# A fused attention, mixer and FFN kernel: centring in three passes, the low part of the sum of squares apart, one inverse root moved

## The chip, the cores and the metric

The kernel runs on one core of a Trainium2 chip, as one launch. The metric is the device time in microseconds (us); lower is better. The engines are called PE (TensorE, matrix products), DVE (VectorE), ACT (ScalarE), POOL (GpSimd) and SP (SyncE, which issues all the transfers here).

## The reference

Three layers follow one another. The first is a delta-rule attention over 4 batches, 8 heads and 768 tokens, the second a token mixer, the third an FFN behind a layer norm. The change lies in the second and third:

```python
# mixer: x is the attention's output, [4, 768, 384]
theta = x @ w_theta
y = einsum('ts,bsd->btd', w_tok_r, x * cos(theta)) + einsum('ts,bsd->btd', w_tok_i, x * sin(theta))
u = x + y
x = u + maximum(u @ w_ch, 0)
# FFN
mu = mean(x, axis=-1); var = mean((x - mu) ** 2, axis=-1)
xn = (x - mu) / sqrt(var + 1e-06) * g_ln
out = x + maximum(xn @ w_ch1, 0) @ w_ch2          # 384 -> 1536 -> 384
```

## The kernel before

The matrix products keep nearly full precision with a rounded high part and a low part (the rest) of both operands: high times high, low times high, high times low. So each operand is split first: ACT copies (rounds) the high part, DVE (or POOL) subtracts it from the original to get the low part.

**The mixer** runs 24 iterations, one for each pair of batch and token tile in `MIX` (L1410 to L1445). An iteration i first multiplies sine and cosine of the next one with x on DVE (`turn`, L1071), rounds the product on ACT (L1072) and makes its low part on DVE (`rest`, L1078); then comes the first half of its own token product (`mix(i, 0)`, L1097, 18 matmuls), the angles of iteration i + 2 (`theta`, 9 matmuls, L1037; `transpose` of i + 3, L970; `angles`, `sines`, `cosines`), and the second half (`mix(i, 1)`, 18 matmuls). At the last iteration of a group, 20 and 23 among them, each half ends in three evictions of PSUM on DVE (L1107), and the next group's products can only begin in those buffers after them. Between these stand stages of the weights (`wts.pump`).

**The FFN** works in 8 blocks j of 384 tokens. Ahead of a block stands a list of steps, made by `pre` (L1137 to L1204), which the loops call one by one: `parts` (index 0: split of u), `ch` three times (1 to 3: a channel piece, 9 matmuls L1155, and its eviction L1157), `total(u, "m")` (4: the sum over three tiles, L1162 and L1163, with its high part on ACT, L1166, and its low part on DVE, L1167), `centre` (5: two matmuls with ones, L1173, spread the mean over all partitions in PSUM; then for each of three tiles a subtraction on DVE, L1182, an ACT copy, L1121, and a low part on DVE, L1122), `square` (6: squares on ACT, L1189, and again `total`), and `rstd` (7: two matmuls L1173, then L1196 DVE, L1197 ACT root, L1198 DVE reciprocal, L1199 DVE, L1200 POOL, L1201 DVE). For block 0 all of this runs in the mixer's iterations 15 to 22 (L1415, L1444); for a later block inside the block before it (`first` for block 0's own loop, `later` for the others, L1459, L1460), with `rstd` at step f = 3 of the block itself (L1465).

The loop of the FFN (L1461 to L1476) has 12 steps f to a block. A step issues `up` (9 matmuls L1214, ReLU on ACT L1218, the hidden tile's low part on DVE L1219), then a pump, then the steps of the next block's list, and then `down` (9 matmuls L1233) for the step two earlier. So a hidden tile is due two steps after its up. The order in the program is the order on each engine; nothing overtakes on DVE, ACT, POOL or SP.

**The weights** come through `pump` (L807 to L826). f0 to f8 were prepared earlier and stored in DRAM; they are loaded as they are (L789), rounded on ACT (L911), and their low part is made half on POOL and half on DVE (L918; the half of `up` is POOL's). f9 to f11 are loaded raw (L785): magnitude on ACT (L880), four DVE operations (L886, L887, L896, L897), a scale on POOL (L830), and then the same L911 and L918. Each of these is a stage that a pump advances by one; the last of them are done in block 0. A load waits until an earlier stage frees its buffer: f3's is behind the low part of f0.

```python
def split(self, raw, hi, lo, parts):                       # L1118
    for p in parts:
        nc.scalar.copy(out=hi[:, p], in_=raw[:, p])
        nc.vector.tensor_tensor(out=lo[:, p], in0=raw[:, p], in1=hi[:, p].bitcast(F32), op=ALU.subtract)
```

Of the kernel before, what the change touches and what calls it, by code (L numbers as in the profile page):

```python
# [6 lines left out]
F32 = mybir.dt.float32  # L7
# [4 lines left out]
ALU = mybir.AluOpType  # L12
# [720 lines left out]
C = 384  # L733
KB = 3
NT_ = 6
NF = 12
N = 384
NJ = 8
# [373 lines left out]
class FFN:  # L1112
# [24 lines left out]
    def pre(self, j, big, wp, psc):  # L1137

        nc = self.nc
        u = self.view(j)  # L1140
        hold = {}

        def parts():
            uh = big("uh", F32R)
            ul = big("ul", F32R)
            self.split(u, uh, ul, range(KB))
            hold["u"] = uh, ul

        def ch(e):
            uh, ul = hold["u"]  # L1150
            ps = psc.tile([128, N], F32, name="pc", tag="pa")
            n = 0
            for w, r in ((0, uh), (1, uh), (0, ul)):
                for k in range(KB):
                    nc.tensor.matmul(ps, self.wc[w][:, k, 128 * e:128 * e + 128], r[:, k], start=(n == 0), stop=(n == 8))  # L1155
                    n += 1
            nc.vector.scalar_tensor_tensor(out=u[:, e], in0=ps, scalar=0.0, in1=u[:, e], op0=ALU.max, op1=ALU.add)  # L1157

        def total(src, key):
            t = wp.tile([128, N], F32, name="tot")  # L1160
            e = nc.vector if j <= 1 and key == "m" else nc.gpsimd
            e.tensor_tensor(out=t, in0=src[:, 0], in1=src[:, 1], op=ALU.add)  # L1162
            e.tensor_tensor(out=t, in0=t, in1=src[:, 2], op=ALU.add)  # L1163
            sh = self.sp.tile([128, N], F32R, name="sh")
            sl = self.sp.tile([128, N], F32R, name="sl")
            nc.scalar.copy(out=sh, in_=t)  # L1166
            nc.vector.tensor_tensor(out=sl, in0=t, in1=sh.bitcast(F32), op=ALU.subtract)  # L1167
            hold[key] = sh, sl

        def bcast(key):  # L1170
            ps = psc.tile([128, N], F32, name="pst", tag="pa")
            for n, r in enumerate(hold[key]):
                nc.tensor.matmul(ps, self.ones, r, start=(n == 0), stop=(n == 1))  # L1173
            return ps

        def centre():
            ps = bcast("m")
            xc = big("ul", F32)
            xh = big("xh", F32R, j)
            xl = big("xl", F32R, j)  # L1180
            for k in range(KB):
                nc.vector.scalar_tensor_tensor(out=xc[:, k], in0=ps, scalar=-1.0 / C, in1=u[:, k], op0=ALU.mult, op1=ALU.add)  # L1182
                self.split(xc, xh, xl, (k,))
            self.XC[j] = xh, xl
            hold["xc"] = xc

        def square():
            sq = big("uh", F32)
            nc.scalar.activation(out=sq, in_=hold["xc"], func=AF.Square)  # L1189
            total(sq, "v")  # L1190

        def rstd():
            ps = bcast("v")
            t = lambda nm, p=wp: p.tile([128, N], F32, name=nm)
            v, a, y = t("v"), t("tot"), t("rs", self.rp if j else self.rp0)
            nc.vector.tensor_scalar(out=v, in0=ps, scalar1=1.0 / C, scalar2=1e-6, op0=ALU.mult, op1=ALU.add)  # L1196
            nc.scalar.activation(out=y, in_=v, func=AF.Sqrt)  # L1197
            nc.vector.reciprocal(out=y, in_=y)  # L1198
            nc.vector.scalar_tensor_tensor(out=a, in0=v, scalar=0.5, in1=y, op0=ALU.mult, op1=ALU.mult)  # L1199
            nc.gpsimd.tensor_tensor(out=a, in0=a, in1=y, op=ALU.mult)  # L1200
            nc.vector.scalar_tensor_tensor(out=y, in0=a, scalar=1.5, in1=y, op0=ALU.subtract, op1=ALU.mult)  # L1201
            self.RS[j] = y

        return [parts, lambda: ch(0), lambda: ch(1), lambda: ch(2), lambda: total(u, "m"), centre, square, rstd]  # L1204

    def up(self, j, f, wp, psh):
        nc = self.nc
# [60 lines left out]
def build(tc, a):  # L1268
    nc = tc.nc
# [3 lines left out]
    for n in ("wth", "wtok", "wch", "wff"):  # L1273
        t = a[n]
        a[n] = t.bitcast(U32).rearrange("... (n t) -> ... n t", t=2) if wide else t

    with tc.manual_schedule(), outer:
# [12 lines left out]
        wts = Weights(nc, None, wide)  # L1290
# [80 lines left out]
        def stash(fs):  # L1371
            for f in fs:
                flat[f] = dp.tile([128, 2, C], F32, name=f"flat{f}")
                wts.stash(("s", f), a["wff"][f], flat[f], g)
# [3 lines left out]
        def two_f(f, hi, lo):  # L1378
            for n in range(2):
                kept = f + n < KEPT  # L1380
                ff.load_f(f + n, flat if kept else a["wff"], hi[:, 2 * n:2 * n + 2], lo[:, 2 * n:2 * n + 2], wts,
                          None if kept else g)
# [14 lines left out]
        wp = Late()  # L1397
        todo = first_pre = ff.pre(0, big, wp, psa)
        ff.rp0 = lp
        mx.trans(DELAY)  # L1400
        for i in range(n):
            b, s = MIX[i]
            assert ("w", s, 1) in wts.ready
            if i + 1 < n:
                mx.turn(i + 1)
            if i == 0:
                mx.rest(1)
            for _ in range(PA[i]):
                wts.pump()
            if 0 < i < n - 1:  # L1410
                mx.rest(i + 1)
            mx.mix(i, 0, yp)
            for _ in range(PB[i]):
                wts.clamps()
            for k in {16: (1,), 17: (2,), 18: (3,), 22: (7,)}.get(i, ()):  # L1415
                todo[k]()
            if i + DELAY < n:
                mx.theta(i + DELAY)
            if i + DELAY + 1 < n:
                mx.transpose(i + DELAY + 1)  # L1420
            if i + DELAY < n:
                mx.angles(i + DELAY)
            if i + DELAY + 1 < n:
                mx.copies(i + DELAY + 1)
            if i + DELAY < n:
                mx.sines()
                mx.cosines()
            for _ in range(PB[i]):
                wts.pump()
            mx.mix(i, 1, yp)  # L1430
            if i == 3:
                wts.more = None
            if i == 6:
                spare.close()
                ff.load_ch(a["wch"], outer.enter_context(tc.tile_pool(name="wch", bufs=1)), wts)
                stash(range(KEPT))
            if i == 21:
                two_f(0, *[slot(f"f0_{k}", 6 + k, [128, 4, C], F32R) for k in range(2)])
            if i == 22:
                two_f(2, *[slot(f"f2_{k}", 4 + k, [128, 4, C], F32R) for k in range(2)])  # L1440
            assert i < 15 or ("c", 2) in wts.ready, wts.todo
            if i == 15:
                wp.pool = ff.sp = Spare(mx.cst, ("w1_0", "w1_1"))
            for k in {15: (0,), 18: (4,), 19: (5,), 20: (6,)}.get(i, ()):  # L1444
                todo[k]()  # L1445
# [10 lines left out]
            two_f(f, *[fp.tile([128, 4, C], F32R, name=f"f{f}_{k}") for k in range(2)])  # L1456
        items = [(j, f) for j in range(NJ) for f in range(NF)]
        LAG = 2
        first = {3: (0,), 5: (1,), 6: (2,), 7: (3, 4), 9: (5,), 10: (6,)}  # L1459
        later = {1: (0,), 2: (1,), 3: (2,), 4: (3, 4), 7: (5,), 8: (6,)}  # L1460
        for i in range(len(items)):  # L1461
            j, f = items[i]
            if f == 0:
                last, todo = todo, ff.pre(j + 1, big, wp, psa) if j + 1 < NJ else None
            if j and f == 3:  # L1465
                last[7]()
            wts.until(("f", f))
            ff.up(j, f, hp, yp)
            for _ in range(2 if (j, f) == (0, 4) else 1):
                wts.pump()  # L1470
            if j + 1 < NJ:
                for k in (later if j else first).get(f, ()):
                    todo[k]()
            if i >= LAG:
                j, f = items[i - LAG]
                ff.down(j, (f,), yp)  # L1476
# [34 lines left out]
```

## Time and profile before

| | |
|---|---|
| time, median of 3 runs | 757.25 us (755.95 to 758.97) |
| the profiled execution | 758.89 us, of it 757.1 us span |
| busy: PE, DVE, ACT, POOL | 714.7 us (94%), 513.7 us (68%), 337.7 us (45%), 198.7 us (26%) |
| mean granted clock of PE | 0.984 of full speed |

The span is the time from the first to the last instruction of the profiled execution; what lies around it is 1.8 us. The attention takes about the first 210 us, the mixer runs until 407 us, and the FFN from there to the end. The profile names the engine, the line and the operation of each instruction, `out<-in` by the program's tiles (in the mixer the small tiles of `pre` lie in spare weight tiles and are called `w`), and in brackets how long the engine stood idle ahead of it and what released it.

### The profile page before, as it was taken

The page shows a single profiled execution, that of the slowest core. Times are in us where ns is not written, and L with a number is a line of the kernel's source. Part 1 is how long each engine was busy: PE and PEld are TensorE (multiplying, and loading weights), DVE is VectorE, ACT ScalarE, POOL GpSimd, SP SyncE. Part 2 cuts the span into 40 slices and gives each one's busy share as a digit, 9 for nine tenths or more (in the row PEclk, how much of TensorE's full clock was granted, in tenths as well). Part 3 has the DMA queues.
Part 4 walks back from the last instruction along what each step waited for, and adds up shares of the span by engine and source line. Part 5 has one row for each costly group of instructions (what it writes and reads, how often), then busy time and mean ns, then how long its engine had stood idle before and what let it go on. Part 6 is the DMA issues. An engine that isn't in the chain of part 4 may idle for free.

```text
span 757.1 us, 19286 instructions
## 1 busy us (share of the span) xinstructions
PE 714.7 (94%) x8188; PEld 655.0 (87%) x8188; DVE 513.7 (68%) x861; ACT 337.7 (45%) x718; POOL 198.7 (26%) x224
## 2 busy tenths in 40 slices
PE   5688889998999999999989989999999999999997
PEld 3466566665799999999978989999999999999997
DVE  8998989999978899887857765344443635344332
ACT  2376767886576675544444532322313232221211
POOL 2866756561010002111014332111221312111110
PEclk7699999999999999999999999999999999999999
DMA  8997867455433122543212400000000000000000
GB/s 233 290 233 180 204 172 196 124 142 157 135 130 110 59 63 87 163 126 95 95 63 83 168 1 32 1 31 1 3 31 1 32 1 31 1 32 1 1 32 32
DMA packets 29671, 67.56 MB, mean 89 GB/s; under 512 B 5136, under 2 KB 17808, under 8 KB 29584
## 3 DMA queue, kind: packets, MB, share of 16 engines
q1 hardware_dynamic: 29584, 66.33, 30.2%
q8 instruction: 64, 1.05, 0.6%
q14 instruction: 23, 0.19, 0.1%
HBM read 53.33 MB, written 8.26 MB: 81 GB/s over the span
## 4 chain that ended last, share of the span: by engine, by line
PE 72%; DVE 13%; issue 5%; DMA 4%; POOL 3%; ACT 3%; SPq 0%; ACTq 0%; POOLq 0%; DVEq 0%
PE acc L1233 18%; PE ph L1214 18%; PE y L1097 15%; PE pth L1037 4%; PE pc L1155 4%; DMA bdk<-kq 2%; PE pa L187 2%; PE S L500 2%; DVE prod L397 2%; PE W L486 1%; PE py L535 1%; DVE XT L406 1%; DMA raw<-wff 1%; DVE t L896 1%; PE py L515 1%
## 5 line engine op out<-in xcount | busy, mean ns | idle before, releaser
L1097 PE MATMUL y<-w,zh 128*128 128x384 f32 x576 | 153.6, 340 | 2.0 <-ACT zh L1072 1.0
L1233 PE MATMUL acc<-hh,f 128*128 128x384 f32 x576 | 147.6, 337 | 0.7 <-ACT hh L1218 0.7
L1219 DVE SCALAR_TENSOR_TENSOR hl<-ph,hh 128x384 fp32r<-128x384 f32 x96 | 52.5, 554 | 108.0 <-ACT hh L1218 106.6
L1214 PE MATMUL ph<-xh,f 128*128 128x384 f32 x576 | 117.2, 338 | 0.6 <-DVE u L1107 0.6
L1218 ACT ACTIVATE hh<-ph 128x384 fp32r<-128x384 f32 x96 | 46.7, 491 | 153.7 <-PE ph L1214 151.9
L1097 PEld LDWEIGHTS y<-w,zh 128*128 128x128 f32 x576 | 104.6, 188 | 2.8 <-ACT zh L1072 1.3
L1233 PEld LDWEIGHTS acc<-hh,f 128*128 128x128 f32 x576 | 104.7, 188 | 1.0 <-ACT hh L1218 1.0
L1214 PEld LDWEIGHTS ph<-xh,f 128*128 128x128 f32 x576 | 102.7, 189 | 0.8 <-issue 0.8
L1097 PE MATMUL y<-w,zl 128*128 128x384 f32 x288 | 97.2, 337 | 0.6 <-DVE zl L1078 0.6
L1233 PE MATMUL acc<-hl,f 128*128 128x384 f32 x288 | 97.4, 338 | 0.0
L1214 PE MATMUL ph<-xl,f 128*128 128x384 f32 x288 | 65.7, 336 | 0.0
L1097 PEld LDWEIGHTS y<-w,zl 128*128 128x128 f32 x288 | 54.1, 188 | 1.2 <-DVE zl L1078 1.0
L1233 PEld LDWEIGHTS acc<-hl,f 128*128 128x128 f32 x288 | 54.3, 189 | 0.3 <-DVE hl L1219 0.3
L505 ACT COPY bds<-S 48x384 f32<-48x384 f32 x92 | 43.6, 474 | 23.9 <-PE S L500 22.2
L1214 PEld LDWEIGHTS ph<-xl,f 128*128 128x128 f32 x288 | 51.6, 188 | 0.0
L1243 POOL TENSOR_TENSOR o<-u,o 128x384 f32<-128x384 f32 x21 | 20.8, 1018 | 87.0 <-DVE o L1242 87.0
L492 ACT COPY bdw<-W 128x384 f32<-128x384 f32 x96 | 41.4, 482 | 4.2 <-PE W L486 3.0
L500 PE MATMUL S<-bdw,ktt 128*48 128x192 f32 x368 | 40.3, 337 | 0.0
L187 PE MATMUL pa<-bdk,kqt 128*32 128x128 f32 x640 | 27.1, 302 | 10.9 <-DMA bdk<-kq 3.5
L486 PEld LDWEIGHTS W<-Rs,pt 32*32 32x32 f32 x1472 | 19.2, 105 | 19.1 <-ACT Rs L474 10.6
L830 POOL TENSOR_TENSOR t<-t,g 128x384 f32<-128x384 f32 x12 | 14.2, 1180 | 75.7 <-DVE t L897 66.9
L187 PEld LDWEIGHTS pa<-bdk,kqt 128*32 128x32 f32 x640 | 20.0, 121 | 13.4 <-issue 7.8
(198 smaller groups left out, 1308.6 us busy)
## 6 DMA issues: line engine op xcount, KB each, us to landing
raw<-wff SPq DMA_DIRECT2D x12, 768.0 KB, 5.1
bdk<-kq SPq DMA_DIRECT2D x40, 192.0 KB, 5.2
raw<-wtok SPq DMA_DIRECT2D x7, 768.0 KB, 4.4
vt<-vin SPq DMA_DIRECT2D x24, 192.0 KB, 5.0
ktt<-ktok SPq DMA_DIRECT2D x24, 192.0 KB, 5.6
kqt<-kq SPq DMA_DIRECT2D x24, 192.0 KB, 4.1
x<-ys SPq DMA_DIRECT2D x96, 48.0 KB, 3.7
out<-o SPq DMA_DIRECT2D x24, 192.0 KB, 1.9
```

What stands on the lines that cost most here:

```text
L187: nc.tensor.matmul(hold[0][32 * r:32 * r + 32, g, :, :].rearrange("p e (k i) -> p e k i", k=2), KQ[c][:, 0, g, r, :], bdk[c % 2][:, :, :, ...
L486: nc.tensor.matmul(W_ps[j // 2][rr, j % 2, r, :], PT[c // 4][rr, (m0 + j) // 2, :, j % 2], Rs[rr, j, :], start=True, stop=True)
L492: nc.scalar.copy(out=b[:, 2 * k:2 * k + 2], in_=W_ps[k])
L500: nc.tensor.matmul(S_ps[h][64 * e:64 * e + D, g, :], KT[c][:, 2 * h + g, e, :], b[:, 2 * g + e, :, :], start=(c == 0 and g == 0), stop=Tru ...
L505: nc.scalar.copy(out=n[ee, :, e, :], in_=S_ps[h][ee, :, :].rearrange("p g (r d) -> p (g r) d", r=4))
L1037: nc.tensor.matmul(ps, l[:, k], self.tw[w][:, k], start=(n == 0), stop=(n == 8))
L1097: nc.tensor.matmul(self.Y[q], l[:, ri, 128 * k:128 * k + 128], self.W[s][w][:, 2 * ri + h], start=(first and w == ri == 0 and l is zh), st ...
L1155: nc.tensor.matmul(ps, self.wc[w][:, k, 128 * e:128 * e + 128], r[:, k], start=(n == 0), stop=(n == 8))
L1214: nc.tensor.matmul(ps, w[:, 0, 128 * k:128 * k + 128], r[:, k], start=(n == 0), stop=(n == 8))
L1218: nc.scalar.activation(out=hh, in_=ps, func=AF.Relu)
L1219: nc.vector.scalar_tensor_tensor(out=hl, in0=ps, scalar=0.0, in1=hh.bitcast(F32), op0=ALU.max, op1=ALU.subtract)
L1233: nc.tensor.matmul(self.ACC[j][e], w[:, 1, 128 * e:128 * e + 128], r, start=(f == 0 and n == 0), stop=(f == NF - 1 and n == 2))
```

## The change

The change has four parts. `total` is cut into the sum (`total`) and the split of the sum (`fold`). `centre` subtracts the mean from all three tiles first and then splits all three. `rstd` is cut into `spread` (the broadcast and one DVE operation) and `rstd` (root, reciprocal and the correction step); the tiles `rs` and `v` change roles. So the list of `pre` has ten steps: 4 `mean` (sum and split of the mean), 5 `centre`, 6 `square` (squares and their sum only), 7 the split of the sum of squares, 8 `spread`, 9 `rstd`.

The places of the steps change too. Block 0's steps: 7 after the first half-mix of iteration 21, 8 after the first half-mix of iteration 22 (where `rstd` stood), 9 in the FFN at f = 2 of block 0. Block 1's steps in block 0: `mean` one step later (f = 8, after it stood with the third channel piece at f = 7), `centre` at 10, `square` at 11, and each ahead of the pump, not behind it. Later blocks: step 7 at f = 2 and steps 8 and 9 at f = 3 of the block itself, behind the up and the next block's piece, not ahead of the up.

```diff
@@ total
             e.tensor_tensor(out=t, in0=src[:, 0], in1=src[:, 1], op=ALU.add)
             e.tensor_tensor(out=t, in0=t, in1=src[:, 2], op=ALU.add)
+            hold[key] = t
+
+        def fold(key):
+            t = hold[key]
             sh = self.sp.tile([128, N], F32R, name="sh")
             sl = self.sp.tile([128, N], F32R, name="sl")
             nc.scalar.copy(out=sh, in_=t)
@@ centre
             for k in range(KB):
                 nc.vector.scalar_tensor_tensor(out=xc[:, k], in0=ps, scalar=-1.0 / C, in1=u[:, k], op0=ALU.mult, op1=ALU.add)
-                self.split(xc, xh, xl, (k,))
+            self.split(xc, xh, xl, range(KB))
@@ rstd
+        def spread():
+            ps = bcast("v")
+            v = (self.rp if j else self.rp0).tile([128, N], F32, name="rs")
+            nc.vector.tensor_scalar(out=v, in0=ps, scalar1=1.0 / C, scalar2=1e-6, op0=ALU.mult, op1=ALU.add)
+            hold["v"] = v
+
         def rstd():
-            ps = bcast("v")
-            t = lambda nm, p=wp: p.tile([128, N], F32, name=nm)
-            v, a, y = t("v"), t("tot"), t("rs", self.rp if j else self.rp0)
-            nc.vector.tensor_scalar(out=v, in0=ps, scalar1=1.0 / C, scalar2=1e-6, op0=ALU.mult, op1=ALU.add)
+            v = hold["v"]
+            y = wp.tile([128, N], F32, name="v")
+            a = wp.tile([128, N], F32, name="tot")
             nc.scalar.activation(out=y, in_=v, func=AF.Sqrt)
             nc.vector.reciprocal(out=y, in_=y)
             nc.vector.scalar_tensor_tensor(out=a, in0=v, scalar=0.5, in1=y, op0=ALU.mult, op1=ALU.mult)
             nc.gpsimd.tensor_tensor(out=a, in0=a, in1=y, op=ALU.mult)
-            nc.vector.scalar_tensor_tensor(out=y, in0=a, scalar=1.5, in1=y, op0=ALU.subtract, op1=ALU.mult)
-            self.RS[j] = y
-
-        return [parts, lambda: ch(0), lambda: ch(1), lambda: ch(2), lambda: total(u, "m"), centre, square, rstd]
+            nc.vector.scalar_tensor_tensor(out=v, in0=a, scalar=1.5, in1=y, op0=ALU.subtract, op1=ALU.mult)
+            self.RS[j] = v
+
+        def mean():
+            total(u, "m")
+            fold("m")
+
+        return [parts, lambda: ch(0), lambda: ch(1), lambda: ch(2), mean, centre, square, lambda: fold("v"), spread, rstd]
@@ the mixer's loop
-            for k in {16: (1,), 17: (2,), 18: (3,), 22: (7,)}.get(i, ()):
+            for k in {16: (1,), 17: (2,), 18: (3,), 21: (7,), 22: (8,)}.get(i, ()):
                 todo[k]()
@@ the FFN's loop
-        first = {3: (0,), 5: (1,), 6: (2,), 7: (3, 4), 9: (5,), 10: (6,)}
+        first = {3: (0,), 5: (1,), 6: (2,), 7: (3,), 8: (4,), 10: (5,), 11: (6,)}
         later = {1: (0,), 2: (1,), 3: (2,), 4: (3, 4), 7: (5,), 8: (6,)}
...
-            if j and f == 3:
-                last[7]()
             wts.until(("f", f))
             ff.up(j, f, hp, yp)
-            for _ in range(2 if (j, f) == (0, 4) else 1):
-                wts.pump()
-            if j + 1 < NJ:
-                for k in (later if j else first).get(f, ()):
+            if j == 0:
+                for k in first.get(f, ()):
                     todo[k]()
+                for _ in range(1 + (f == 4)):
+                    wts.pump()
+            elif j + 1 < NJ:
+                for k in later.get(f, ()):
+                    todo[k]()
+            for k in ({2: (9,)} if j == 0 else {2: (7,), 3: (8, 9)}).get(f, ()):
+                last[k]()
             if i >= LAG:
                 j, f = items[i - LAG]
                 ff.down(j, (f,), yp)
```

## Rows read from the trace of the kernel before

**Rows 1.** Stretches: window, length, busy of PE PEld DVE ACT POOL, clock, DMA.
```profile
380.00:395.00 15.00, 12.61 (x69) 11.74 (x69) 9.20 (x16) 6.82 (x12) 2.03 (x2) 1.00 0.13 47
500.00:600.00 100.00, 100.00 (x574) 100.00 (x573) 46.85 (x80) 25.35 (x52) 20.07 (x20) 1.00 0.05 19
```

**Rows 2.** PE's waits from 210 us on: total, times, longest.
```profile
PE pst L1173 <- ACT sh L1166: 2.0, 1, 2.0
PE y L1097 <- ACT zh L1072: 1.0, 1, 1.0
PE y L1097 <- DVE u L1107: 0.8, 1, 0.8
PE pt L970 <- DVE ul L1182: 0.8, 1, 0.8
PE acc L1233 <- ACT hh L1218: 0.7, 1, 0.7
PE ph L1214 <- DVE u L1107: 0.6, 1, 0.6
PE y L1097 <- DVE zl L1078: 0.6, 1, 0.6
```

**Rows 3.** Timeline, PE, end of the mixer: start, us, engine, line, operation, tiles.
```profile
373.23 0.52 PE L1173 MATMUL pst<-w,ones 128*128 128x384 f32 x2
...
376.76 1.20 PE L1037 MATMUL pth<-tw,xh 128*128 128x384 f32 x6
...
407.39 1.30 PE L1214 MATMUL ph<-xh,f 128*128 128x384 f32 x6 [0.56 <-DVE u L1107]
```

**Rows 4.** A stretch behind the wait at 442 us; the chain of waits there.
```profile
444.00:445.00 1.00, 1.00 (x5) 1.00 (x4) 0.89 (x2) 0.08 (x1) 0.82 (x1) 0.50 0.00 0
...
443.34 2.41 PE acc L1233 x9
```

**Rows 5.** Timeline, DVE, mixer iterations 20 to 22.
```profile
375.44 0.55 DVE L1182 SCALAR_TENSOR_TENSOR ul<-pst,u 128x384 f32<-128x384 f32 x1
...
380.26 0.95 DVE L1071 TENSOR_TENSOR zf<-zf,x 128x768 f32<-128x768 f32 x1
...
383.06 1.48 DVE L1107 TENSOR_TENSOR u<-u,y 128x384 f32<-128x384 f32 x3
...
390.45 0.56 DVE L1167 TENSOR_TENSOR w<-w,w 128x384 fp32r<-128x384 f32 x1 [3.12 <-ACT w L1166]
```

**Rows 6.** Timeline, ACT and DVE, block 0's inverse root.
```profile
397.83 1.28 ACT L1197 ACT_TABLE_LOAD   x1
...
399.86 2.55 DVE L1198 RECIPROCAL rs<-rs 128x384 f32<-128x384 f32 x1 [0.59 <-ACT rs L1197]
...
402.45 0.56 DVE L1199 SCALAR_TENSOR_TENSOR w<-w,rs 128x384 f32<-128x384 f32 x1
...
404.13 1.34 DVE L1201 SCALAR_TENSOR_TENSOR rs<-w,rs 128x384 f32<-128x384 f32 x1 [1.13 <-POOL w L1200]
...
405.40 1.38 DVE L918 TENSOR_TENSOR f<-t,f 128x384 fp32r<-128x384 f32 x1
```

**Rows 7.** Timeline, ACT, the FFN's first two ReLUs.
```profile
412.46 0.87 ACT L1218 ACTIVATE hh<-ph 128x384 fp32r<-128x384 f32 x2 [1.50 <-POOL f L918]
```

**Rows 8.** Stretches of block 0 (columns as rows 1); timeline, ACT, block 1's mean.
```profile
413.00:426.00 13.00, 12.99 (x73) 12.70 (x74) 7.62 (x13) 7.84 (x14) 6.82 (x5) 1.00 0.65 241
...
417.20:442.85 25.65, 23.57 (x134) 22.99 (x132) 20.61 (x32) 10.80 (x19) 9.35 (x8) 1.00 0.31 118
...
441.74 0.51 ACT L1166 CAST sh<-tot 128x384 fp32r<-128x384 f32 x1 [5.98 <-DVE tot L1163]
```

**Rows 9.** Timeline, DVE and POOL: splits in blocks 0 and 1, f10's half.
```profile
418.44 2.31 DVE L1122 TENSOR_TENSOR ul<-u,uh 128x384 fp32r<-128x384 f32 x3
...
439.99 1.30 POOL L918 TENSOR_TENSOR f<-t,f 128x384 fp32r<-128x384 f32 x1
...
458.63 1.49 DVE L1122 TENSOR_TENSOR ul<-u,uh 128x384 fp32r<-128x384 f32 x3
```

## The prediction, on record before the changed kernel ran

> **What bounds the kernel now.** I read the stretches first: in the FFN's later blocks TensorE (PE) is busy for the whole of 500 to 600 us, 574 matmuls in 100 us, 0.174 us each, so nine of them (one "piece": an up, a down or a channel piece) take 1.57 us; between 380 and 395 us it is busy for only 12.6 of 15 us [rows 1]. So the second half of the span is PE bound, and an edit can only gain where PE stands still. Then I read PE's own waits from 210 us on: eight, all before 443 us, five of them in the last mixer iterations (0.8, 0.8, 1.0, 0.6, 0.6, together 3.7), two in the first FFN block (0.7 and 2.0; an eighth of 0.2 is left out of the rows) [rows 2]. Everything the change touches lies around these. Each wait costs more than its idle time, because the pipeline refills, so I measure the loss by pace: from the end of the two broadcast matmuls at 373.23 to the theta at 376.76 PE does 2 + 18 matmuls in 3.53 us, 0.1765 each. From 376.76 to the first FFN matmul there are 2 thetas of 9, seven half-mixes of 18 and 2 broadcast matmuls, 146 in all: 25.8 us, and 0.25 us for a transpose, so 402.8 instead of 407.39 [rows 3]. The mixer's tail loses 4.6 us. In the first FFN block, from 407.4 to 443.2 are 20 pieces and a broadcast: 31.4 + 0.35 = 31.75 us of work in 35.8 us, 4.0 lost; and behind the 2.0 us wait the granted clock is 0.50 (1.2 GHz instead of 2.4) and a piece takes 2.41 us; two such pieces lose another 1.6 [rows 4]. All that can be won is 4.6 + 5.6 = 10.2 us.
>
> **Centring in three passes** (block 0, after iteration 19). Before, three subtractions from the broadcast alternate with ScalarE copies, so VectorE (DVE) runs from 375.44 to 380.26 before the next turn [rows 5]. Three back-to-back operations of this size take 1.49 us [rows 9]; three subtractions and then three low parts need 2 x 1.49 = 3.0 us, the copies running beside them: 378.4, 1.8 earlier. The PSUM buffer is free after the first pass, at 376.95, before PE asks (378.3): the 0.8 us wait at the transpose goes. The evictions that start at 383.06 [rows 5] start at 381.2, the first ends 0.55 later, at 381.8, just as PE arrives (376.76 + 27 x 0.1765 + 0.25): I take 0.3 of the second 0.8 us as left. In later blocks the three passes lie beside a busy PE: nothing.
>
> **The sum of squares split.** The low part waited 3.12 us on DVE (it starts at 390.45), with the next turn queued behind it [rows 5]. Now the GpSimd (POOL) sum stays at the end of iteration 20 and the copy and low part come after half a mix of iteration 21, behind the turn. The turn comes 3.1 + 0.56 + 1.8 = 5.5 us earlier, more than the waits of 1.0 and 0.6 us that it ended [rows 2]. The copy can hold ScalarE (ACT) until POOL is done, ahead of the next angles; those have the 5.5 us.
>
> **The inverse root of block 0 moved.** Out of the mixer go a table load of 1.28 us on ACT, and on DVE everything from the reciprocal at 399.86 (2.55) to the last step, which starts at 404.13 after a POOL wait of 1.13 and takes 1.34: 5.6 us [rows 6]. The weight low part at 405.40 and the evictions behind it move up by as much, so the first up's wait of 0.6 us goes, and so does the load of f3, which SP issues only when that low part is done (406.8); the chain load, ACT copy, POOL low part ended at 412.46 in the first ReLU and cost PE 0.7 us [rows 2, 7]. All moved steps stay ahead of PE's new arrival at 402.8. Mixer: 4.6 - 0.3 = 4.3 us won.
>
> It goes to step f = 2 of the FFN, behind that step's ReLU and weight copy. From the first up, PE ends up 2 after 0.1 + 3 x 1.57 = 4.8 us; ReLU 0.65 with its delay, copy 0.8, table load 1.28, root 0.53: DVE can begin at +8.1 and is held by reciprocal 2.55, product 0.56, POOL 1.1, last step 0.56 until +12.9 [rows 6]. Queued behind it on DVE are the low half of f3's hidden tile and the split for the channel pieces. The hidden half is done at +13.4 and due in the fourth down, behind ten pieces, at +15.8; the split (1.5 us without POOL beside it, 2.3 with [rows 9]) ends at +14.9 to +15.7; its first third is due in channel piece 0 at +0.1 + 9 x 1.57 + 1.05 = +15.3, its last at +15.6, and the first is done by +14.2. Without that cover PE would wait there, microsecond for microsecond.
>
> **The order in the first block.** DVE is the second bound: idle 5.4 of the 13 us up to 426, then so full that ACT waits 5.98 us for its total, until 441.74, and PE for ACT [rows 2, 8]. The moved root puts 4.9 us into that idle time. Does it fit? From 417.20 until the mean's low part ended (442.85) DVE was busy 20.6 us [rows 8]. The same work now starts at +12.9, with one more hidden half in front (0.5) and the ACT copy's round trip (0.6): the low part ends at +34.6. The mean's broadcast moves from after up 9 to after up 10; in front of it stand 22 pieces: +0.1 + 34.5 = +34.6. A tie, where the kernel before was 2.1 late. The pieces ahead of weight stages cost nothing in sum: they change the order on DVE, and the last halves of f10 are POOL's, which ended at 441.3 [rows 9], 1.55 ahead of the mean's low part; the same now is +33.05, needed after three matmuls of up 10 at +33.6. I take 0.5 us of waits for these close places, no clock fall (that followed a wait of 2.0; waits of up to 1.0 left the clock at 1.00 [rows 1, 2]) and 0.3 us of refills. First block: 5.6 - 0.8 = 4.8 us won.
>
> **Later blocks.** The root comes a step's up later, behind the channel piece; the same five operations hold DVE about 5 us, and a hidden half is due four pieces, 6.3 us, after its up. PE waits in none of these blocks now, and I put this at nothing; without that cover each block would pay up to the difference, seven times, under 1 us each.
>
> **Two rules weighed.** The trace shows the table load at 1.28 us with the root following within 0.2 [rows 6]. The Trainium skill, ScalarE: Activation LUTs, section What ACT_TABLE_LOAD costs, states the same load but adds a drain of 1.38, 2.66 together. By that figure the root would end 1.4 us later and the tie become a wait of 1.4; the trace disagrees and decides. The same page, section Table sets: the hidden batching unit, says that cheap functions such as ReLU are in every set; no run here shows ReLU under the sine table.
>
> **Rivals.**
> A. The mean is still late. With DVE 2 us later than summed (the turn of two engines, contention), PE waits 2 us and the clock falls: 748.2 + 2 + 1.6 = 751.8. For it: the tie has no slack. Chance 0.20.
> B. The root takes back what the mixer gains. If POOL and ACT put all of its 4.9 us behind the idle time, the broadcast is 5 late, f10 and f11 too, with two falls of the clock: first-block loss 5 + 0.5 + 3.2 = 8.7 against 5.6: 757.25 - 4.3 + 3.1 = 756. Against it: 5.4 us idle in front. Chance 0.10.
> C. The change doesn't do what it says: the evictions stay the last wait, the split is ordered by something else, and the mixer gives 1.5 only: 757.25 - 1.5 - 4.8 = 751. Chance 0.06. If neither part works: no change, 757; chance 0.03.
> D. Slower, by contention. The last step beside POOL took 1.34 and the three low parts 2.31, where without POOL the product of the same shape took 0.56 and the three 1.49 [rows 6, 9]: up to 0.8 us for each DVE operation with two SBUF inputs. Between +8 and +34.6 DVE has some 18 such; if the new order laid POOL beside all, DVE would be 14 us late: 757.25 - 4.3 - 5.6 + 14 + 1.6 = 763. It decides from 11 to 12 such meetings on (slower by 0.5%). POOL has only eight operations there, so few meet. Chance 0.04.
> The Trainium skill, GPSIMD Engine Reference, section 8. Key points, says that GpSimd shares its SBUF interfaces with VectorE and contends with instructions of two SBUF inputs; by that rule D is the way, and the trace agrees with 1.34 against 0.56.
>
> **How the numbers follow.** Forecast: 4.3 + 4.8 = 9.1 us off. Against the profiled execution (758.89, span 757.1) that is 749.8 and a span of 748.0; against the median of 757.25 it is 748.2. Its chance is 0.57, A 0.20, B 0.10, C 0.06, D 0.04, nothing 0.03. The range runs from all 10.2 won, less 1.3 for the spread of the runs, 745.8, to A with half of the 1.7 by which the slowest run lies over the median, 752.6. 0.5% is 3.8 us (about what a measurement of this kernel can tell from no change), so faster is under 753.5: forecast, A and C, 0.83; within: B and nothing, 0.13; slower: D, 0.04.
>
> **What would show it.** Right: no PE wait in the last mixer iterations above 0.3 us; the first up at 403 in the trace's time; the root's five operations around +8 to +13 after it; the broadcast after up 10 with under 1 us of wait; granted clock 1.00 from 440 to 450; no new PE wait from block 1 on. Wrong: a PE wait on the mean, or on a weight half of f9 to f11, of 2 us or more; a channel piece waiting for its split; a second table load; a wait at the hidden halves of f3 to f5.

## The result, and the profile after

The changed kernel took 748.73 us in the median against 757.25 us, a ratio of 0.989 (95% interval 0.9863 to 0.9917). That is 8.5 us faster; the forecast was 748.2. The execution that was profiled first took 2414 us with PE slow from end to end and shows nothing of the change; all lines of the changed kernel below are from another execution with a span of 748.0 us (the label `after_again`), where the same comparison gave 0.989 (0.9844 to 0.9936).

The first 370 us, which the change doesn't touch, differ from one execution to the next by up to 6 us. So I compare two stretches inside one trace: from the broadcast of block 0's mean (the first `pst` matmul) to the first `up`, and from there to the end of the span. Two traces of one kernel agree in their sum within 0.2 us.

| kernel | mean's broadcast to first up | first up to end | sum |
|---|---|---|---|
| before, two traces | 34.16, 34.28 | 349.71, 349.71 | 383.87, 383.99 |
| changed, two traces | 29.34, 29.43 | 345.86, 345.84 | 375.20, 375.27 |

The change brought 4.8 us in the mixer's tail and 3.9 us behind it, 8.7 us together. PE's waits from 230 us on, which filled eight lines before [rows 2], are one line now (total, times, longest), and the first up comes at 402.14:

```profile
PE pc L1155 <- DVE ul L1122: 0.8, 1, 0.8
```

The timeline of PE (start, duration, engine, line, operation) at the two ends of the first stretch, as in [rows 3]:

```profile
372.80 0.52 PE L1177 MATMUL pst<-w,ones 128*128 128x384 f32 x2
...
402.14 1.20 PE L1227 MATMUL ph<-xh,f 128*128 128x384 f32 x6
```

The timeline of DVE in iterations 20 to 22, answering to [rows 5]: three subtractions and three low parts stand in one block of 2.9 us, the turn follows at 377.80, and the next turn (384.79) comes ahead of the low part of the sum of squares, which now waits 1.45 us without making PE wait behind it.

```profile
375.00 1.48 DVE L1186 SCALAR_TENSOR_TENSOR ul<-pst,u 128x384 f32<-128x384 f32 x3
376.40 1.49 DVE L1122 TENSOR_TENSOR xl<-ul,xh 128x384 fp32r<-128x384 f32 x3
377.80 0.95 DVE L1071 TENSOR_TENSOR zf<-zf,x 128x768 f32<-128x768 f32 x1
...
380.61 1.48 DVE L1107 TENSOR_TENSOR u<-u,y 128x384 f32<-128x384 f32 x3
...
384.79 0.95 DVE L1071 TENSOR_TENSOR zf<-zf,x 128x768 f32<-128x768 f32 x1
...
389.11 0.56 DVE L1171 TENSOR_TENSOR w<-w,w 128x384 fp32r<-128x384 f32 x1 [1.45 <-ACT w L1170]
```

The timelines of ACT, DVE, POOL and PE in the first FFN block, answering to [rows 6, 8, 9]. The root stands at f = 2: its reciprocal starts 8.0 us after the first up. Its last step again meets POOL (1.36 us, where 0.56 was taken in the forecast), the split of u behind it takes 2.65 us beside POOL's three low parts, and channel piece 0 waits for it. The mean's low part is done at 437.85, its broadcast follows at 438.10 without a wait.

```profile
408.25 1.28 ACT L1206 ACT_TABLE_LOAD   x1
...
410.11 2.55 DVE L1207 RECIPROCAL v<-v 128x384 f32<-128x384 f32 x1 [1.28 <-ACT v L1206]
...
414.32 3.59 POOL L918 TENSOR_TENSOR f<-t,f 128x384 fp32r<-128x384 f32 x3
...
414.39 1.36 DVE L1210 SCALAR_TENSOR_TENSOR rs<-tot,v 128x384 f32<-128x384 f32 x1 [1.14 <-POOL tot L1209]
415.68 0.55 DVE L1232 SCALAR_TENSOR_TENSOR hl<-ph,hh 128x384 fp32r<-128x384 f32 x1
416.15 2.65 DVE L1122 TENSOR_TENSOR ul<-u,uh 128x384 fp32r<-128x384 f32 x3
...
416.22 1.22 PE L1155 MATMUL pc<-uh,wc 128*128 128x384 f32 x6
417.28 0.34 PE L1155 MATMUL pc<-ul,wc 128*128 128x384 f32 x1
418.38 0.91 PE L1155 MATMUL pc<-ul,wc 128*128 128x384 f32 x2 [0.76 <-DVE ul L1122]
...
437.29 0.56 DVE L1171 TENSOR_TENSOR sl<-tot,sh 128x384 fp32r<-128x384 f32 x1 [0.58 <-ACT sh L1170]
...
438.10 0.34 PE L1177 MATMUL pst<-sh,ones 128*128 128x384 f32 x1
```

Stretches (window, length, busy of PE, PEld, DVE, ACT, POOL, granted clock, DMA): behind the mean's broadcast the clock is 1.00 where it had been 0.50 [rows 4]. From the start of the ninth down to the end of the span PE was busy 305.02 us in the changed kernel (second row) and 305.02 us in the kernel before (last row), so the later blocks cost PE nothing. The two windows differ by 0.3 us all the same: the span ends that much later behind the last operation.

```profile
440.00:450.00 10.00, 10.00 (x59) 10.00 (x58) 4.71 (x10) 5.20 (x10) 2.03 (x2) 1.00 0.00 0
...
438.45:748.00 309.55, 305.02 (x1746) 304.70 (x1745) 137.01 (x234) 76.06 (x152) 55.38 (x55) 1.00 0.05 16
...
447.88:757.10 309.22, 305.02 (x1746) 304.70 (x1745) 131.27 (x228) 75.45 (x150) 54.28 (x54) 1.00 0.05 16
```

The 0.3 us lie in the closing of the program, in SP's waits for PE's queue (SP's waits in the last 7 us: total, times, longest; the kernel before, then the changed one):

```profile
SPq L1507 <- PEq L1507: 0.6, 2, 0.4
...
SPq L1523 <- PEq L1523: 0.9, 2, 0.7
```

Both traces of either kernel show it so. Why it is longer isn't shown. So from the first up to the ninth down the change brought 4.2 us (36.3 instead of 40.5), and 0.3 of them went again at the end.

### The profile page after: what moved, and what is told of

It reads as the page before. It is cut to its first block, busy times and chain, and to the rows that moved or that the text cites. A ratio compares the mean times of both kernels' runs of the same rounds, so it can differ in the third digit from the quotient of the medians.

```text
span 2412.5 us, 19286 instructions
## 1 busy us (share of the span) xinstructions
PE 2398.3 (99%) x8187; PEld 1574.4 (65%) x8188; DVE 512.5 (21%) x861; ACT 347.1 (14%) x718; POOL 185.6 (8%) x224
## 4 chain that ended last, share of the span: by engine, by line
PE 99%; DVE 0%; DMA 0%; issue 0%; ACT 0%; POOL 0%; SPq 0%; DVEq 0%; ACTq 0%; POOLq 0%
PE acc L1246 22%; PE y L1097 22%; PE ph L1227 22%; PE pth L1037 6%; PE pc L1155 6%; PE S L500 5%; PE pa L187 3%; PE py L535 2%; PE W L486 2%; PE R L467 2%; PE py L515 2%; PE R L471 2%; PE pt L970 1%; PE pst L1177 1%; PE py L588 0%; DMA kqt<-kq 0%
## 5 line engine op out<-in xcount | busy, mean ns | idle before, releaser
L1097 PE MATMUL y<-w,zh 128*128 128x384 f32 x576 | 445.6, 898 | 0.0
L1246 PE MATMUL acc<-hh,f 128*128 128x384 f32 x576 | 433.8, 889 | 0.0
L1227 PE MATMUL ph<-xh,f 128*128 128x384 f32 x576 | 381.0, 889 | 0.0
L1227 PEld LDWEIGHTS ph<-xh,f 128*128 128x128 f32 x576 | 243.4, 423 | 111.5 <-issue 89.2
L1246 PEld LDWEIGHTS acc<-hh,f 128*128 128x128 f32 x576 | 244.3, 424 | 110.0 <-issue 87.1
L1097 PEld LDWEIGHTS y<-w,zh 128*128 128x128 f32 x576 | 243.8, 423 | 109.3 <-issue 81.8
L1097 PE MATMUL y<-w,zl 128*128 128x384 f32 x288 | 256.1, 889 | 0.0
L1246 PE MATMUL acc<-hl,f 128*128 128x384 f32 x288 | 255.4, 887 | 0.0
L1227 PE MATMUL ph<-xl,f 128*128 128x384 f32 x288 | 203.3, 890 | 0.0
L1155 PE MATMUL pc<-uh,wc 128*128 128x384 f32 x144 | 95.5, 895 | 0.0
```

Of the source, the lines that this page charges most:

```text
L1097: nc.tensor.matmul(self.Y[q], l[:, ri, 128 * k:128 * k + 128], self.W[s][w][:, 2 * ri + h], start=(first and w == ri == 0 and l is zh), st ...
L1227: nc.tensor.matmul(ps, w[:, 0, 128 * k:128 * k + 128], r[:, k], start=(n == 0), stop=(n == 8))
L1246: nc.tensor.matmul(self.ACC[j][e], w[:, 1, 128 * e:128 * e + 128], r, start=(f == 0 and n == 0), stop=(f == NF - 1 and n == 2))
```

## The experiments

My theory was that the four parts each remove their own waits and that DVE, in order and nearly full in the first block, decides what is left. The rivals were that one part does all, that the root takes back in the FFN what it gives in the mixer, and that the order of the pieces does nothing by itself. Each run leaves one part out, does one part alone, or moves or doubles one cost. The two stretches of every trace (the sum of the changed kernel is 375.2):

| kernel | to first up | to the end | sum | against changed | median of its runs |
|---|---|---|---|---|---|
| `centre_by_tile` | 31.34 | 346.10 | 377.44 | +2.2 | 751.81 |
| `low_with_sum` | 33.06 | 345.73 | 378.79 | +3.6 | 751.15 |
| `root_in_mixer` | 30.47 | 345.49 | 375.96 | +0.8 | 749.97 |
| `order_before` | 29.43 | 348.16 | 377.59 | +2.4 | 751.13 |
| `pump_first` | 29.39 | 346.58 | 375.97 | +0.8 | 750.07 |
| `order_alone` | 35.15 | 344.92 | 380.07 | +4.9 | 752.65 |
| `recip_twice` | 29.48 | 349.91 | 379.39 | +4.2 | 752.13 |
| `root_after_centre`, two traces | 29.34, 29.44 | 344.92, 344.99 | 374.26, 374.43 | -0.9 | 748.53, 748.13 |

The times of the kernel before were 756.05 to 756.48 beside all of these. The sums tell differences apart to about 0.2 us, the medians to about 2 us. Two sums, `low_with_sum` and `order_alone`, hold a fall of the clock worth 1.5 us, which may not come in each execution.

Undone one at a time, the four parts (the first four rows) cost 2.2, 3.6 with that fall of the clock, 0.8 and 2.4 us. So no part does all.

### The changed kernel itself, twice

No edit.

> The changed kernel itself, once more, for a profile with a fast PE. The forecast: a span near 748.0 us less the 757.1 of before's scale, so 746 to 748; the first up at about 403 us; no PE wait above 0.3 us between 376 us and the first up; the mean's broadcast (after up 10 of block 0) with 0 to 1 us of wait; granted clock 1.00 behind it. Rival A (the mean still late): a wait of about 2 us there and a fall of the clock, and then the mixer would have given more than summed. Rival B: weight halves f10, f11 or channel piece 0 waited for as well.

Measured: span 748.0, 748.21 us in the median, no wait before the first up, the broadcast without a wait; but channel piece 0 waited 0.76 us. Rival A didn't come: PE didn't wait for the mean. Of rival B one piece came, the wait of channel piece 0; no weight half was waited for. Beside the last version below, once more:

> The changed kernel again, beside the next one on one chip. 748 to 749, from the first up to the end 345.9 us in the trace.

Measured: 747.82 us, and 345.84 us from the first up to the end.

### Centring by tile again

```diff
             for k in range(KB):
                 nc.vector.scalar_tensor_tensor(out=xc[:, k], in0=ps, ...)
-            self.split(xc, xh, xl, range(KB))
+                self.split(xc, xh, xl, (k,))
```

> The changed kernel with centring undone to subtract, copy, low part tile by tile. My theory: DVE is 1.8 us later in iteration 20, the wait of 0.8 us at the transpose and most of the 0.8 us at the evictions return, about 1.6 to 2.0 us with refills, all of it before the first up; so 1.0022 to 1.0027 of the changed kernel, 750.4 to 750.7. Rival: PE's waits were set by the low part and the root, and centring alone changes less than 0.5 us.

Measured: 2.0 us more in the first stretch, 0.2 behind it. The median of 751.81 us lies 1.1 us above the theory's, which is within what the medians tell apart. Two of PE's waits of before are back, at the sizes they had [rows 2]:

```profile
PE y L1097 <- DVE u L1107: 0.8, 1, 0.8
PE pt L970 <- DVE ul L1186: 0.8, 1, 0.8
```

So the order of six DVE operations is worth 2.0 us there: 0.8 + 0.8 idle, which leaves 0.2 each for the refills.

### The low part back beside its sum

```diff
         def square():
...
             total(sq, "v")
+            fold("v")
...
-        return [parts, ..., mean, centre, square, lambda: fold("v"), spread, rstd]
+        return [parts, ..., mean, centre, square, lambda: None, spread, rstd]
```

> The changed kernel with the copy and the low part of the sum of squares back behind the squares, ahead of the next turn, for all blocks. My theory: the turn of iteration 22 starts when the low part is done, about 389.6 on the changed kernel's scale instead of 384.8, its copy ends 1.8 us later, and PE, which asks at 389.3, waits about 2 us for it and half a us for its low part: 2.3 to 3.0 us slower, all between the mean's broadcast and the first up (29.3 becomes 31.6 to 32.3). Rival: three-pass centring gives the POOL sum enough lead, and PE waits under 0.5 us.

Measured: 33.06 instead of 29.34 us in the first stretch, 3.7 more, where 2.3 to 3.0 were expected. The waits are those of before, 1.02 and 0.55 us (timeline of PE), and behind them the granted clock was 0.57 on the mean of 4 us (the stretch below; at the lower level 0.50, 1.2 GHz instead of 2.4): some ten matmuls came 0.32 us apart instead of 0.175, 1.5 us of the 3.7. The other 2.2 are the waits with their refills. My theory had 2 us for the first wait, twice what came, and no fall of the clock. The POOL sum's lead didn't do away with the waits, so the rival falls.

```profile
387.04 0.44 PE L1097 MATMUL y<-w,zh 128*128 128x384 f32 x1 [1.02 <-ACT zh L1072]
388.03 0.44 PE L1097 MATMUL y<-w,zl 128*128 128x384 f32 x1 [0.55 <-DVE zl L1078]
...
388.00:392.00 4.00, 3.97 (x14) 3.97 (x15) 1.40 (x2) 2.41 (x5) 0.00 (x0) 0.57 0.01 4
```

### The root back in the mixer

```diff
-            for k in {16: (1,), 17: (2,), 18: (3,), 21: (7,), 22: (8,)}.get(i, ()):
+            for k in {16: (1,), 17: (2,), 18: (3,), 21: (7,), 22: (8, 9)}.get(i, ()):
...
-            for k in ({2: (9,)} if j == 0 else {2: (7,), 3: (8, 9)}).get(f, ()):
+            for k in ({} if j == 0 else {2: (7,), 3: (8, 9)}).get(f, ()):
```

> The changed kernel with block 0's root, reciprocal and correction put back into mixer iteration 22. My theory: the wait of the first up for the evictions (0.6) and that of the first down for the ReLU (0.7) return, with refills 1.5 to 1.9 us; the mean's broadcast in block 0 then has DVE time to spare and loses its remaining wait (0 to 0.7): in sum 0.8 to 1.9 us slower. Rival: the root costs the first block as much as it cost the mixer, so the time stays within 0.5 us, and the wait only sits at another place.

Measured: 1.1 us more in the first stretch, 0.4 less behind it, 0.8 in sum. Both waits are back, as PE's waits show, and channel piece 0's is gone:

```profile
PE ph L1227 <- DVE u L1107: 1.0, 1, 1.0
PE acc L1246 <- ACT hh L1231: 0.4, 1, 0.4
```

It lies at the lower edge of my theory, between it and the rival: at f = 2 the root costs PE 1.3 us (channel piece 0 takes 2.91 us instead of 1.57) and saves about 2 (1.1 ahead of the first up, and 0.9 at the first down, its wait with the refill).

### The order of the first block, without and alone

```diff
-        first = {3: (0,), 5: (1,), 6: (2,), 7: (3,), 8: (4,), 10: (5,), 11: (6,)}
+        first = {3: (0,), 5: (1,), 6: (2,), 7: (3, 4), 9: (5,), 10: (6,)}
...
             if j == 0:
-                for k in first.get(f, ()):
-                    todo[k]()
                 for _ in range(1 + (f == 4)):
                     wts.pump()
+                for k in first.get(f, ()):
+                    todo[k]()
```

> The changed kernel with the first block's list in the places of before: the mean with the third channel piece at f = 7, centring at 9, squares at 10, each behind the pump. My theory: DVE is full, the mean's low part can't come before about +34 us after the first up, and the broadcast then asks at +31.5: a PE wait of 2 to 3 us and behind it about 3 us at half clock (1.6 us lost), together 4 to 5 us slower, about 753. Rival: the wait of before came from the late start of the weights in the first block, which the shorter mixer tail mends, and the order costs less than 1 us.

Measured: 2.4 us slower, not 4 to 5. The timeline of PE at the mean's broadcast:

```profile
434.33 0.44 PE L1177 MATMUL pst<-sh,ones 128*128 128x384 f32 x1 [1.17 <-ACT sh L1170]
434.92 0.44 PE L1177 MATMUL pst<-sl,ones 128*128 128x384 f32 x1 [0.15 <-DVE sl L1171]
...
430.00:440.00 10.00, 8.68 (x48) 8.11 (x48) 9.01 (x16) 4.87 (x9) 3.76 (x3) 1.00 0.01 2
```

The wait came back at the place foretold, but with 1.2 us, and the clock stayed at 1.00 (the last row). The term I had left out is the wait at channel piece 0 (0.9 us here): the piece takes 3.37 us instead of 1.57 and sets PE back by 1.8 us ahead of the mean, so DVE was that much less late.

The same order put alone into the kernel before (the reverse of that diff, the rest as it was):

> The kernel before with the new order in block 0 alone (mean at f = 8, centring at 10, squares at 11, pieces ahead of the pump); root, low part and centring as before. My theory: all of the mixer's waits stay (34.2 us from the mean's broadcast to the first up), and the broadcast of block 1's mean asks 3.1 us later, so its 2.0 us wait and the 1.6 us behind it at half clock go: 3.5 to 4 us faster than before, about 753.5. Rival: DVE itself is later by as much with the hidden half in front, and 1 us or more of wait stays, with or without the fall of the clock: under 2 us faster.

Measured: from the first up to the end 344.92 us instead of 349.71, 4.8 us; no wait is left in the first block. The first stretch was 35.15 us, 0.9 longer than before though nothing in it had changed. There too the clock fell behind the two waits of 1.01 and 0.55 us:

```profile
391.00:396.00 5.00, 4.45 (x15) 4.19 (x16) 2.40 (x4) 2.87 (x6) 0.00 (x0) 0.66 0.01 3
```

Not all of the 4.8 us is the order's. The timeline of ACT has the first ReLU:

```profile
410.69 0.87 ACT L1218 ACTIVATE hh<-ph 128x384 fp32r<-128x384 f32 x2 [1.51 <-DMA t<-flat]
```

It starts 39.4 us after the mean's broadcast (371.33) and started 39.2 us after it in the kernel before [rows 3, 7], but PE comes to the first up 0.9 us later, so the first down's wait of 0.7 us for that ReLU is gone here without the order's doing. The sum of both stretches is 3.9 us shorter than before, inside the 3.5 to 4 of my theory.

With the pieces at their new steps, but behind the pump:

```diff
             if j == 0:
-                for k in first.get(f, ()):
-                    todo[k]()
                 for _ in range(1 + (f == 4)):
                     wts.pump()
+                for k in first.get(f, ()):
+                    todo[k]()
```

> The changed kernel with the pump ahead of the pieces again in block 0, but the pieces at their new steps. My theory: the order changes which of DVE's operations comes first and not their sum, so the mean's low part is as late as it was (0 to 0.5 us later against the broadcast), but the split of u comes behind the low part of f6 too and channel piece 0 waits 0.5 to 1.5 us more: 0.5 to 2 us slower than the changed kernel. Rival: the order of pump and pieces is what removed the wait for the mean; then that wait returns with 2 us and the clock falls, 3.5 us slower.

Measured: 0.8 us slower in the trace. The wait of channel piece 0 is 0.92 us instead of 0.76 and lies one matmul earlier in the piece (which takes 3.36 us instead of 2.91), and the mean's low part ends at 438.60, 0.1 us behind the point where PE would take it. So most of the order's gain, 1.6 of 2.4 us, is the later place of the pieces, the mean's above all; the pieces ahead of the pump are worth the remaining 0.8.

### One reciprocal more

```diff
+            if j == 0:
+                nc.vector.reciprocal(out=a, in_=y)
             nc.vector.reciprocal(out=y, in_=y)
```

The added result is overwritten by the product that follows; the output is the same.

> The changed kernel with one more reciprocal (2.55 us on DVE, its result thrown away) in block 0's root at f = 2. My theory: DVE is full from there on, so the split of u is 2.6 us later and channel piece 0 waits 3.2 to 3.6 us instead of 0.8; that long a wait lets the clock fall and two pieces behind it lose some 1.6 us: 4 to 4.5 us slower than the changed kernel. The mean's low part is 2.6 us later too, but PE comes later by as much, and no second wait appears. Rival: DVE finds idle time behind the root and makes up for the reciprocal; then under 1.5 us slower, without a fall of the clock.

Measured: 4.1 us more from the first up to the end. Channel piece 0 waits 2.18 + 0.83 us (timeline of PE), the granted clock falls to 0.50 (a stretch of 2 us behind it), and no second wait appears:

```profile
419.17 0.45 PE L1155 MATMUL pc<-ul,wc 128*128 128x384 f32 x1 [2.18 <-DVE ul L1122]
420.44 1.10 PE L1155 MATMUL pc<-ul,wc 128*128 128x384 f32 x2 [0.83 <-DVE ul L1122]
...
422.00:424.00 2.00, 2.00 (x8) 2.00 (x7) 1.98 (x5) 1.52 (x3) 0.00 (x0) 0.50 0.00 0
```

2.55 us of DVE work at this place became 2.2 us more of waiting, and 1.8 us more went to the clock and the refills. DVE made up for 0.3 us at most.

### The root where DVE has time

```diff
-            for k in ({2: (9,)} if j == 0 else {2: (7,), 3: (8, 9)}).get(f, ()):
+            for k in ({10: (9,)} if j == 0 else {2: (7,), 3: (8, 9)}).get(f, ()):
```

> The changed kernel with block 0's root not at f = 2 but at f = 10 of block 0, behind centring of block 1, where DVE has time. In the changed kernel channel piece 0 waited 0.76 us for the split of u and took 2.91 us instead of 1.57. My theory: that wait is the root's 5.6 us on DVE in front of the split, and POOL's three low parts that came late with it; without the root there the split is done some 5 us before it is due, the wait goes and no other takes its place (the mean's low part is then 3 to 5 us ahead of its broadcast, and a hidden half has 6.3 us, more than the root's 5 to 6): 1.2 to 1.4 us faster than the changed kernel, from the first up to the end 344.5 instead of 345.9. Rival: the split is late because ACT's copies and POOL's low parts of f4 to f6 are late by themselves; then the wait stays, and the root makes a hidden half late at f = 11: slower by 0 to 2 us.

Measured: 344.92 us from the first up to the end, 0.9 less than the changed kernel (1.2 to 1.4 expected). The split of u takes 1.49 us and ends at 412.28, 3.6 us before channel piece 0 begins (415.86). PE reaches the mean's broadcast 34.6 us after the first up instead of 36.0, the 1.3 us that were expected; 0.4 us go again in one short wait with its refill, for a hidden half behind the moved root. The root's last step has no POOL operation beside it here and takes 0.56 us instead of 1.36 (timeline of DVE; PE's waits):

```profile
410.79 1.49 DVE L1122 TENSOR_TENSOR ul<-u,uh 128x384 fp32r<-128x384 f32 x3
...
441.54 2.55 DVE L1207 RECIPROCAL v<-v 128x384 f32<-128x384 f32 x1 [1.01 <-ACT v L1206]
...
445.82 0.56 DVE L1210 SCALAR_TENSOR_TENSOR rs<-tot,v 128x384 f32<-128x384 f32 x1 [1.13 <-POOL tot L1209]
...
PE acc L1246 <- DVE hl L1232: 0.2, 1, 0.2
```

> The changed kernel with block 0's root at f = 10, again. In its first trace channel piece 0 no longer waited and the stretch from the first up to the end was 344.9 us against 345.9. My theory: 1.0 us (0.13%) faster than the changed kernel in the trace, from the mean's broadcast to the end 374.2 to 374.4 against 375.2; in the times that is under what they tell apart, 0.5 to 1.5 us. Rival: the hidden half that came 0.2 us late at f = 11 grows in other executions and eats the gain.

Measured: the sum 374.43, the same 0.2 us wait. It is the shortest of all in the trace, by 0.9 us; its times (748.13 against 747.82 beside it) don't tell it from the changed kernel. So it isn't shown to be faster in time.

### The kernel before, once more

> The kernel before, for one more profile. In the first its two waits at the head of iteration 22 (1.0 and 0.55 us, under 1 us apart) left the granted clock at 1.00; with the same two waits it fell to half for 3 us behind them in two variants. My theory: the waits are the same here (1.0 and 0.55), and whether the clock falls differs from execution to execution: from the mean's broadcast to the first up 34.2 us without a fall, 35.6 to 35.8 with one. Rival: the clock stays at 1.00 for this kernel and something else in the variants lets it fall.

Measured: the same two waits (1.0 and 0.6), 34.28 us to the first up and no fall of the clock. My theory isn't shown: two traces of the kernel before kept the clock, one trace each of `order_alone` and `low_with_sum` lost it behind waits of the same size. What tells them apart stays open.

## Why the prediction was right, point by point

The time lay 0.5 us above the forecast and inside the range; the sums in the trace came to 8.7 us, against 9.1. Two misses of opposite sign and 0.3 us at the end of the span lie in that difference: +0.5 in the mixer, -0.6 in the first block.

- **Mixer's tail:** 4.3 forecast, 4.8 measured. The pace rule (4.6 us lost [rows 3]) was right to 0.2 us: from the theta (376.34) to the first up PE needed 25.8 us, 0.1750 for a matmul where the sum had 0.1765. (373.23 is where the two broadcast matmuls start, not where they end as the prediction words it; its count of 2 + 18 fits the start.) The 0.3 us that I left for the evictions didn't appear: they start at 380.61 and PE doesn't wait. The turn behind the low part came 5.5 us earlier by the sum: it starts 12.0 us after the mean's broadcast (384.79 and 372.80) where it had started 17.7 us after it (390.92 and 373.23), 5.7 earlier.
- **Centring:** forecast at 1.8 us of DVE time and two waits; undoing it alone brought both waits back, 2.0 us.
- **The root's places:** it was foretold to start 8.1 us after the first up and started at 8.0; undone, its 5.6 us in the mixer and the f3 chain cost 1.1 us ahead of the first up and 0.9 us (0.4 of it waiting) at the first down.
- **The first block:** 4.8 forecast, 4.2 measured up to the ninth down (3.9 to the end of the span). The mean's low part was summed to +34.6 us and came at +35.7 us; PE asked at +36.0, because channel piece 0 had held it for 1.3 us. With PE there at the summed +34.6 it would have waited 1.1 us. That the broadcast found its operand ready isn't to the sum's credit but luck: DVE's lateness had held PE too, at piece 0 (`recip_twice` shows the pair again, larger, and no wait at the mean). The step that failed is the split of u. I had bounded it at +14.9 to +15.7 and taken the due time as met; it ended at +16.7. Two terms were mis-sized: the root's last step (0.56 taken though the row beside POOL said 1.34 [rows 6]; measured 1.36), and the split beside POOL (2.65, above my upper bound of 2.31). Both meet POOL because the root holds them on DVE until POOL runs its three low parts of f6 to f8: that of f6 queues behind the root's own POOL step, the other two run straight behind it. With the root at f = 10 the split was done (412.28) before POOL began on f6. As an estimate from these rows, without the 0.8 and 1.2 us that the two were longer beside POOL the split would have ended at +14.7, in time for +15.3; no run takes POOL alone away. Piece 0 took 2.91 us, 1.34 more than a piece; that is nearly all of the 1.4 us that the block still loses. By `recip_twice`, DVE's lateness there goes to PE nearly one for one (2.55 us, of which 2.2 came as waiting).
- **The clock:** the fall behind the mean is gone, as forecast, and none came in the first block (granted clock 1.00 from 402 to 450).
- **Later blocks:** at nothing, and PE was busy there for the same 305.02 us. The 0.3 us in the closing of the program stood in no term.
- **The rivals:** A needed the mean 2 us late; the price I gave such a case, 2 us and 1.6 for the clock, is about what `recip_twice` paid. B and D didn't come, though D's mechanism (POOL beside DVE), with the root in front of the split, made the one wait that is left. That wait is one of the signs that the prediction named for being wrong, a channel piece waiting for its split.
- **The rules weighed:** the table load was 1.28 us again and the root followed at once (409.55 after a load that ended at 409.53); no drain is to be seen. The Trainium skill, ScalarE: Activation LUTs, section Table sets: the hidden batching unit, says that ReLU is in every set; this agrees with the trace, where the first ReLUs (from 404.23) run ahead of that load, and the only other loads start at 0.7 and 155.4 us, the second of them for the sines.

## What to carry to other kernels

In a kernel bound by PE, look for what sits in front of the short stalls in the other engines' order: a wait for a third engine in the middle of DVE's queue costs whatever stands behind it. Take such a chain apart and put its waiting half where the next due time is far; when you move one into a stretch that has idle time on the whole, add up the order of that stretch against each due time, not only the first and the last. Compare stretches within one trace when a change is worth less than the run-to-run spread, and read the granted clock of each stretch before its difference is put down to the change.

## What the hardware showed that I had not expected

- Behind two waits of 1.0 and 0.55 us, under 1 us apart, the granted clock fell to 0.50 (1.2 GHz instead of 2.4) for about 3 us in two traces (`low_with_sum`, `order_alone`; 1.5 us lost) and stayed at 1.00 in two others with the same waits (the kernel before). In the forecast I had taken waits of up to 1.0 us as safe.
- The clock stayed at 1.00 behind a wait of 1.17 us, followed by 0.15 (`order_before`), and fell to 0.50 behind 2.18 and 0.83 (`recip_twice`).
- Beside POOL's low parts three DVE low parts took 2.65 us, and the root's last step 1.36; with POOL idle the same operations took 1.49 and 0.56 (`root_after_centre`). The Trainium skill, GPSIMD Engine Reference, section 8. Key points, states that GpSimd shares its SBUF interfaces with VectorE and contends with instructions of two SBUF inputs; the traces agree with 1.36 against 0.56.
